# Chunked attention before two feed-forward layers: two heads of a pair on the two row halves of TensorE, shared key rows, whole-width loads in a new order

## Chip, cores and metric

The kernel runs on one core of one Trainium2 chip. The metric is the device time of the program in microseconds; 1169.55 us is the median of three runs before the change (1168.73 to 1170.94).

## What is computed

Attention over chunks of 32 queries, each of which sees 8 memory rows, 16 positions to the left of its chunk, the chunk and 8 positions to the right; then two feed-forward layers on the 3072 x 512 result.

```
B, H, S, D = 4, 8, 768, 64
for each chunk c of 32 queries:
    k_full = concat(mem_k, k[l_start:r_end]); v_full likewise      # 64 rows away from the ends
    a = softmax(q_c @ k_full.T / sqrt(D));   out[c] = a @ v_full
x = out as (3072, 512)
x = (s * relu(x @ w_in)**2 + b) @ w_out                             # d_ff 2048
h = x @ w_in2;  y = (max(h, 0) + alpha * min(h, 0)) @ w_out2
```

The feed-forward weights come as 64-bit floats.

## The kernel before, in words

**Feed-forward.** The 3072 tokens are six blocks of 512 columns. A hidden slice f (128 of 2048) of one block is a unit: G1 (`g1`, L488) is 12 matmuls of 128x512, four pieces of the model dimension by three products of high and low halves (`xh`, `xl` and the two halves of each weight); G2 (`g2`, L547 for layer 0, L549 for layer 1) is 12 more. In between stand `relu` and `square` (ScalarE, L499, L504), `affine` (VectorE, L510, which reads `sb_sb`, loaded by `consts`), `g_high` (ScalarE, L527) and `g_low` (VectorE, L532). There are 2 x 6 x 16 units. Layer 0 begins with slices 0 to 4 of block 0, then the same slices of block 1, then slices 5 to 15 of both; the first two slices of block 0 are done in two halves of 256 columns (`HALVES = 2`).

**Weights.** Each slice's pair of weights is loaded raw (`load_part`, L206) and converted by two ScalarE and five VectorE instructions (`convert`, L218 to L249), the last of which, L249, writes the low half.

**Attention.** A tile is 128 queries of all eight heads of one batch; there are 24, four to a block. Heads go in four pairs. `scores` (L321): for each pair and chunk one matmul with 128 rows (both heads' 64 dimensions), 32 output partitions and 128 columns; its moving operand `kd` holds the two heads' keys on the block diagonal, with zeros elsewhere that `clear` (L282) writes once per buffer. `values` (L388) has the same form with `vd`. Softmax follows on VectorE and ScalarE (`maxima` L333, `shifted` L342, `exps` L346, `sums`, or for the first eight tiles `exps_by_head` L365), `turn` (L376) transposes the probabilities, `normal` (L394) divides, `turn_x` (L402) transposes the result, and `x_high` (L407) and `x_low` (L412) write the tile's columns of `xh` and `xl`. Tiles 0 to 7 (blocks 0 and 1) are done at the start, one buffer set of three each, the sets partly in weight slots. Tiles 8 to 23 are done during layer 0, each in two visits to TensorE between units: `values` of the tile before with `scores` of this one, and later the two transposes.

**Loads.** `kw` and `vw` are loaded as two transfers of 64 partitions each (L304, L310), since each half goes to its own block of the diagonal; `qt` (L301) and the raw weights are transfers of 128 partitions. Every chunk's key window is stored in full, so neighbouring chunks' windows repeat rows.

**Order.** Nothing is scheduled at run time. `Plan.order` lists the steps once, from written costs (the second argument of `plan.add`), ranks and dependencies; each engine then runs its steps in that order. SyncE (SP), which issues the loads, takes its steps strictly by rank. `EARLY_QK`, `EARLY_V` and `EARLY_PARTS` are the ranks of the first loads.

Of the kernel before, what the change touches and what calls it, by code (L numbers as in the profile page):

```python
# [21 lines left out]
HP = H // 2  # L22
NC4 = P // CH
# [12 lines left out]
HALVES = 2  # L36
SPLIT = 2
SETS = 3
EARLY_QK = (-200, -190, -170, -150, -30, -20, -10, 0)
EARLY_V = (-180, -165, -155, -140, -25, -15, -5, 5)  # L40
EARLY_PARTS = {0: -185, 1: -145, 2: -90, 3: -35, 4: -8}
SET_SLOTS = {1: (10, 11, 12), 2: (13, 14, 15)}
# [23 lines left out]
class Plan:  # L66


    PAST = {"PE": 0.25, "DVE": 0.08, "ACT": 0.12, "POOL": 0.12, "SP": 1.8, "PQ": 2.2}
    RATE = 330e3  # L70
# [12 lines left out]
    def order(self):  # L83
# [14 lines left out]
        while len(done) < len(self.steps):  # L98
# [42 lines left out]
            for o in s.outs:  # L141
                o.n_wait -= 1
                o.ready = max(o.ready, at[e] if e == "PE" == o.engine else s.end)
                if not o.n_wait:
                    open_[o.engine].append(o)
# [5 lines left out]
def tile_chunk_attention_two_ffn(ctx: ExitStack, tc: tile.TileContext, qt, kw, vw, win, wout, s1, b1, alpha, out):  # L151
# [16 lines left out]
    plan = Plan({"ph": 2, "g": 2, "gg": 3, "ao": 2, "pa": 2})  # L168
# [33 lines left out]
    def load_part(layer, f, mats):  # L202
        raw = slot_tile(f, mats, [P, len(mats), BLK, 2], U32, "raw")
        raws[layer, f, mats] = raw
        for n, m in enumerate(mats):
            nc.sync.dma_start(out=raw[:, n].rearrange("p n two -> p (n two)"), in_=(win, wout)[m][layer][f])  # L206

    def convert(layer, f, mats, rank, after):
# [41 lines left out]

        early = EARLY_PARTS.get(f, rank - 60) if layer == 0 else rank - 60
        load = plan.add("SP", 0.45 * n, early + 14 * mats[0], lambda: load_part(layer, f, mats), after, nbytes=n * (1 << 19))
        load_done[key] = load
        c0 = plan.add("ACT", 0.22 + 0.43 * n, rank, magnitude, [load], takes=("ao", key))
        c1 = plan.add("DVE", 0.06 + 0.36 * n, rank, clamp, [c0])
        c2 = plan.add("DVE", 0.06 + 0.37 * n, rank, shift, [c1])
        c3 = plan.add("DVE", 0.16 + 0.55 * n, rank, low, [c2])
        c4 = plan.add("DVE", 0.16 + 0.55 * n, rank, sign, [c3])
        hi = plan.add("ACT", 0.2 + 0.43 * n, rank, high, [c4])
        lo = plan.add("DVE", 0.16 + 0.55 * n, rank, rest, [hi], frees=[key])  # L260
# [7 lines left out]
    first_use = {}  # L268

    def make_set(n):  # L270
        shape = [P, 2, HP, NC4, NKEY], [P, 2, NC4, HP, D]
        if n == 0:
            kd, vd = (work.tile(s, F32, tag=t, name=t) for s, t in zip(shape, ("kd", "vd")))
        else:
            kd, vd = (wpool.tile(s, F32, tag=f"w{f}", name=t) for s, f, t in zip(shape, SET_SLOTS[n], ("kd", "vd")))
            sets[n, "qa"] = wpool.tile([P, 2, HP, P], F32, tag=f"w{SET_SLOTS[n][2]}", name="qa")
        sets[n] = kd, vd

    def clear(n, which, par, eng):
        if n not in sets:  # L280
            make_set(n)
        eng.memset(sets[n][which][par * D:par * D + D, 1 - par], 0.0)  # L282

    def pair_tile(n, which, name):
        if n == 0:
            return work.tile([P, HP, P], F32, tag=f"qa{which}", name=name)
        return sets[n, "qa"][:, which]

    def set_of(i):
        return i % SETS if i < 2 * TPB else 0  # L290

# [3 lines left out]
    def load_qk(i):  # L295
# [6 lines left out]
        for par in range(2):  # L302
            r = slice(par * D, par * D + D)
            nc.sync.dma_start(out=sets[n][0][r, par], in_=kw[i, r])  # L304

    def load_v(i):
        n = set_of(i)
        for par in range(2):
            r = slice(par * D, par * D + D)
            nc.sync.dma_start(out=sets[n][1][r, par], in_=vw[i, r])  # L310

    def bank(i, shape, name):
        tag = f"po{i}" if i < TPB else f"pa{held(('att', i))}"
        return psum.tile(shape, F32, tag=tag, name=name)

    def scores(i):
        kd, qT = sets[set_of(i)][0], state[i]["q"]
        sc = bank(i, [P, HP, 2, NKEY], "sc")
# [5 lines left out]
        state[i]["sc"] = sc  # L324

    def maxima(i):
        sc = state[i]["sc"].rearrange("p a two n -> p (a two) n")
        if i % TB == 0:
            nc.vector.memset(sc[0:CH, :, NM:NM + LEFT], NEG)
        if i % TB == TB - 1:  # L330
            nc.vector.memset(sc[P - CH:P, :, NKEY - RIGHT:NKEY], NEG)
        m = small.tile([P, H], F32, tag="m", name="m")
        nc.vector.tensor_reduce(out=m, in_=sc, axis=AX.X, op=ALU.max)  # L333
        state[i]["m"] = m

    def new_e(i):
        state[i]["e"] = pair_tile(set_of(i), 0, "e").rearrange("p a (two n) -> p a two n", two=2)
        return state[i]["e"].rearrange("p a two n -> p (a two) n")

    def shifted(i):  # L340
        sc = state[i]["sc"].rearrange("p a two n -> p (a two) n")
        nc.vector.tensor_tensor(out=new_e(i), in0=sc,  # L342
                                in1=state[i]["m"].unsqueeze(2).to_broadcast([P, H, NKEY]), op=ALU.subtract)
# [4 lines left out]
    def sums(i):  # L348
        rs = small.tile([P, H], F32, tag="rs", name="rs")
        nc.vector.tensor_reduce(out=rs, in_=state[i]["e"].rearrange("p a two n -> p (a two) n"), axis=AX.X, op=ALU.add)  # L350
        state[i]["rs"] = rs

    def negate(i):
        nm = small.tile([P, H], F32, tag="nm", name="nm")
# [3 lines left out]
    def exps_by_head(i, heads):  # L358
        sc = state[i]["sc"].rearrange("p a two n -> p (a two) n")
        if heads[0] == 0:  # L360
            state[i]["er"] = new_e(i)
            state[i]["rs"] = small.tile([P, H], F32, tag="rs", name="rs")
        e, rs = state[i]["er"], state[i]["rs"]
        for h in heads:
            nc.scalar.activation(out=e[:, h, :], in_=sc[:, h, :], func=ACTF.Exp, scale=SCALE,  # L365
                                 bias=state[i]["nm"][:, h:h + 1], accum_out=rs[:, h:h + 1])
# [6 lines left out]
    def turn(i):  # L373
        pt = bank(i, [P, HP, P], "pt")
        for hp in range(HP):
            nc.tensor.transpose(pt[:, hp, :], state[i]["e"][:, hp, :, :].rearrange("p a n -> p (a n)"), ident)  # L376
# [6 lines left out]
    def values(i):  # L383
        vd, aT = sets[set_of(i)][1], state[i]["aT"]
        px = bank(i, [P, HP, 2 * D], "px")
        for hp in range(HP):
            for c in range(NC4):
                nc.tensor.matmul(px[c * CH:(c + 1) * CH, hp, :], lhsT=aT[:, hp, c * CH:(c + 1) * CH],  # L388
                                 rhs=vd[:, :, c, hp, :], start=True, stop=True)
        state[i]["px"] = px  # L390

    def normal(i):
        xn = pair_tile(set_of(i), 1, "xn")
        nc.vector.tensor_tensor(out=xn.rearrange("p a (two d) -> p (a two) d", two=2),  # L394
                                in0=state[i]["px"].rearrange("p a (two d) -> p (a two) d", two=2),
# [476 lines left out]
```

## Time and profile before

| | |
|---|---|
| median of three runs | 1169.55 us (1168.73 to 1170.94) |
| profiled execution, own time | 1167.94 us |
| its span, first to last instruction | 1166.2 us |
| TensorE busy | 1131.6 us, 97% |
| VectorE busy | 612.0 us, 52% |
| ScalarE busy | 354.8 us, 30% |
| DMA moved | 101.66 MB |

Busy time of TensorE counts overlapping matmuls once; a busy TensorE need not be at its peak. A group's row tells line, engine, operation, output<-input, shape and count. In a timeline a row is one instruction or a run of like ones; the time in square brackets is how long the engine sat idle before it, with what released it.

### The profile page before, as it was taken

How to read it: one execution, taken by the hardware profiler on the slowest of the kernel's cores; microseconds unless marked ns; L12 is line 12 of the kernel's file. 1: busy time of each engine (PE TensorE's matmuls, PEld its weight loads, DVE VectorE, ACT ScalarE, POOL GpSimd, SP SyncE). 2: the span in 40 equal slices, each digit the busy share in tenths (PEclk: the TensorE clock that was granted, in tenths of full speed). 3: DMA queues.
4: the chain of work that ended last, by engine and by line, in shares of the span. 5: the costliest groups of instructions: out<-in, count | busy, mean ns of one | idle time of the engine just before them, and what ended most of it. 6: DMA issues, size and time to landing. Idle time of an engine off the chain costs nothing.

```text
span 1166.2 us, 15335 instructions
## 1 busy us (share of the span) xinstructions
PE 1131.6 (97%) x6384; PEld 932.2 (80%) x6384; DVE 612.0 (52%) x932; ACT 354.8 (30%) x653; POOL 34.1 (3%) x64
## 2 busy tenths in 40 slices
PE   4799999999999999999999999999999999999998
PEld 3678778888888888888888788888888888888886
DVE  6695794455445445444588785433433433434433
ACT  4675554433223223223565331111111111111111
POOL 2000000000000000000000000000000000000000
PEclk9899999999999999999999999999999999999999
DMA  9994204426123123203555402001002102000000
GB/s 241 266 326 170 82 1 138 107 68 177 46 60 123 46 64 113 59 19 109 191 206 204 158 1 73 37 1 72 37 1 72 37 1 73 37 1 1 37 1 37
DMA packets 34613, 101.66 MB, mean 87 GB/s; under 512 B 4592, under 2 KB 4592, under 8 KB 34544
## 3 DMA queue, kind: packets, MB, share of 16 engines
q1 hardware_dynamic: 28848, 80.76, 22.7%
q0 software_dynamic: 5696, 19.93, 4.5%
q8 instruction: 50, 0.82, 0.3%
q14 instruction: 19, 0.16, 0.0%
HBM read 79.70 MB, written 20.97 MB: 86 GB/s over the span
## 4 chain that ended last, share of the span: by engine, by line
PE 48%; issue 44%; DMA 4%; ACT 2%; POOL 1%; DVE 1%; SPq 0%; POOLq 0%; ACTq 0%
PE ph L488 23%; PE po L549 22%; DMA kd<-in_kw_dram 2%; PE po L547 2%; POOL x1d L586 1%; DMA raw<-in_wout_dram 1%; PE px L388 0%; DMA qa<-in_qt_dram 0%; ACT qa L365 0%; ACT e L365 0%; DMA x1d<-o 0%; ACT g L499 0%; ACT a L218 0%; PE sc L321 0%; DMA out_dram<-y 0%
## 5 line engine op out<-in xcount | busy, mean ns | idle before, releaser
L488 PE MATMUL ph<-xh,w 128*128 128x512 f32 (+1 forms) x1552 | 508.4, 390 | 1.6 <-DVE w L249 1.6
L488 PEld LDWEIGHTS ph<-xh,w 128*128 128x128 f32 x1552 | 291.4, 188 | 65.2 <-issue 3.2
L488 PE MATMUL ph<-xl,w 128*128 128x512 f32 (+1 forms) x776 | 301.0, 388 | 0.0
L527 ACT ACTIVATE gh<-g 128x512 fp32r<-128x512 f32 (+1 forms) x194 | 121.7, 627 | 467.5 <-DVE g L519 377.7
L547 PE MATMUL po<-gh,w 128*128 128x512 f32 (+1 forms) x784 | 255.3, 387 | 1.2 <-ACT os L559 1.2
L549 PE MATMUL po<-w,gh 128*128 128x512 f32 x768 | 252.4, 391 | 2.6 <-DVE o L583 2.6
L532 DVE TENSOR_TENSOR gl<-g,gh 128x512 fp32r<-128x512 f32 (+1 forms) x194 | 132.9, 685 | 104.4 <-ACT gh L527 103.8
L514 DVE TENSOR_SCALAR g<-ph,alpha_sb 128x512 f32<-128x512 f32 x96 | 72.0, 750 | 211.0 <-PE ph L488 211.0
L547 PEld LDWEIGHTS po<-gh,w 128*128 128x128 f32 x784 | 146.5, 188 | 32.1 <-issue 1.6
L549 PEld LDWEIGHTS po<-w,gh 128*128 128x128 f32 x768 | 144.9, 189 | 33.2 <-DVE o L583 3.0
L488 PEld LDWEIGHTS ph<-xl,w 128*128 128x128 f32 x776 | 146.4, 189 | 28.6
L547 PE MATMUL po<-gl,w 128*128 128x512 f32 (+1 forms) x392 | 151.1, 385 | 1.4 <-DVE gl L532 1.4
L549 PE MATMUL po<-w,gl 128*128 128x512 f32 x384 | 149.9, 390 | 0.0
L499 ACT ACTIVATE g<-ph 128x512 f32<-128x512 f32 (+1 forms) x98 | 57.9, 591 | 144.8 <-PE ph L488 142.9
L547 PEld LDWEIGHTS po<-gl,w 128*128 128x128 f32 x392 | 73.7, 188 | 16.4 <-DVE gl L532 2.2
L549 PEld LDWEIGHTS po<-w,gl 128*128 128x128 f32 x384 | 72.3, 188 | 15.1
L506 DVE TENSOR_TENSOR g<-g 128x512 f32<-128x512 f32 x48 | 33.3, 693 | 77.5 <-ACT g L499 77.3
L510 DVE TENSOR_SCALAR g<-g,sb_sb 128x512 f32<-128x512 f32 (+1 forms) x98 | 52.4, 534 | 39.7 <-ACT g L504 37.8
L519 DVE SCALAR_TENSOR_TENSOR g<-ph,g 128x512 f32<-128x512 f32 x96 | 66.2, 689 | 2.7
L218 ACT ACTIVATE a<-raw 128x1024 f32<-128x1024 f32 (+1 forms) x36 | 37.4, 1039 | 25.3 <-DVE w L249 10.4
L243 ACT ACTIVATE w<-a 128x1024 fp32r<-128x1024 f32 (+1 forms) x36 | 34.7, 963 | 29.9 <-DVE a L236 29.9
L249 DVE TENSOR_TENSOR w<-a,w 128x1024 fp32r<-128x1024 f32 (+1 forms) x36 | 39.6, 1102 | 4.5 <-ACT w L243 4.4
(64 smaller groups left out, 563.1 us busy)
## 6 DMA issues: line engine op xcount, KB each, us to landing
raw<-in_win_dram SPq DMA_DIRECT2D x32, 512.0 KB, 4.6
raw<-in_wout_dram SPq DMA_DIRECT2D x32, 512.0 KB, 5.7
kd<-in_kw_dram SPq DMA_DIRECT2D x48, 256.0 KB, 4.7
vd<-in_vw_dram SPq DMA_DIRECT2D x48, 256.0 KB, 4.8
x1d<-o POOLq DMA_DIRECT2D x24, 512.0 KB, 3.2
xh<-x1d SPq DMA_DIRECT2D x6, 1024.0 KB, 5.6
xl<-x1d SPq DMA_DIRECT2D x6, 1024.0 KB, 7.6
out_dram<-y POOLq DMA_DIRECT2D x20, 256.0 KB, 2.3
```

The costliest lines, as they stand in the source:

```text
L218: nc.scalar.activation(out=temp["a"], in_=words(1).bitcast(F32), func=ACTF.Abs)
L243: nc.scalar.activation(out=w[:, :, 0, :], in_=temp["a"], func=ACTF.Copy)
L249: nc.vector.tensor_sub(out=w[:, :, 1, :], in0=temp["a"], in1=w[:, :, 0, :].bitcast(F32))
L488: nc.tensor.matmul(p, lhsT=w[:, a, kk * P:(kk + 1) * P], rhs=x[:, kk, cols], start=(i == 0), stop=(i == 3 * KD - 1))
L499: nc.scalar.activation(out=new_g(u), in_=ph.pop(u), func=ACTF.Relu)
L510: nc.vector.tensor_scalar(out=g, in0=g, scalar1=sb_sb[:, 0:1], scalar2=sb_sb[:, 1:2], op0=ALU.mult, op1=ALU.add)
L514: nc.vector.tensor_scalar(out=new_g(u), in0=ph[u], scalar1=0.0, scalar2=alpha_sb[:, f:f + 1], op0=ALU.min, op1=ALU.mult)
L519: nc.vector.scalar_tensor_tensor(out=g, in0=ph.pop(u), scalar=0.0, in1=g, op0=ALU.max, op1=ALU.add)
L527: nc.scalar.activation(out=gh, in_=gt[u], func=ACTF.Copy)
L532: nc.vector.tensor_sub(out=gl, in0=gt.pop(u), in1=gh.bitcast(F32))
L547: nc.tensor.matmul(po[d][:, cols], lhsT=w[:, a, ds_], rhs=g, start=start, stop=stop)
L549: nc.tensor.matmul(po[d], lhsT=g[:, ds_], rhs=w[:, a, :], start=start, stop=stop)
```

## The change

The two heads of a pair become two matmuls of 64 rows and 64 columns each, one on each half of the array's rows, that write to two PSUM banks. Neither `kd` nor `vd` has zeros any more, and `clear` is gone. The key window of four chunks is one row of 184 positions, in which a chunk's right context is the next chunk's left one (before, 256). Keys and values load as one transfer of 128 partitions per tile. There are four buffer sets at the start (two of their own, two in weight slots 14 and 15 with slot 13), and two instead of one afterwards. Tiles 0 to 3 use the four `po` banks in pairs, all others one tile `pa` of two banks. The first loads stand in a written list, the first tiles have other ranks, `exps_by_head` is used for tiles 4 to 7 alone, `HALVES` is 1, and the planner's costs differ.

```diff
-HALVES = 2
+HALVES = 1
-SETS = 3
-EARLY_QK = (-200, -190, -170, -150, -30, -20, -10, 0)
+SETS, OWN_SETS = 4, 2
+FIRST_LOADS = """q0 w0i q1 v0 v1 w0o q3 q2 v3 q4 w1i v2 w2 v4 w3 q5 w1o v5 w6 q6 v7 w4 q7 c v6 w7 w5 w9 w8""".split()
+TILE_RANKS = (-130, -90, -85, -115, 0, -30, -25, -10, 0)
+BY_HEAD = (4, 5, 6, 7)
+KROW = NC4 * (CH + NM) + KHEAD
...
     def load_qk(i):
-        for par in range(2):
-            r = slice(par * D, par * D + D)
-            nc.sync.dma_start(out=sets[n][0][r, par], in_=kw[i, r])
+        nc.sync.dma_start(out=sets[n][0], in_=kw[i])
...
     def scores(i, banks=None):
         for hp in range(HP):
             for c in range(NC4):
-                nc.tensor.matmul(sc[c * CH:(c + 1) * CH, hp, :, :].rearrange("p two n -> p (two n)"),
-                                 lhsT=qT[:, hp, c * CH:(c + 1) * CH], rhs=kd[:, :, hp, c, :],
-                                 start=True, stop=True)
+                for par in range(2):
+                    r = slice(par * D, par * D + D)
+                    nc.tensor.matmul(parts[par][c * CH:(c + 1) * CH, 0, hp, :],
+                                     lhsT=qT[r, hp, c * CH:(c + 1) * CH], rhs=kd[r, hp, c * (CH + NM):c * (CH + NM) + NKEY],
+                                     start=True, stop=True)
...
+    def products(prev, i):
+        banks = bank_pair(i, "sp")
+        if i is not None:
+            scores(i, banks)
+        if prev is not None:
+            values(prev, banks)
```

`values` changes as `scores` does. In the order of instructions this shows at three places. First, TensorE at one attention visit of the later tiles; L388 and L415 are `values`, L321 and L335 `scores`, `po` and `ph` the feed-forward around it. Before:

```order
L547 MATMUL po_2589<-gl,w 128x512
L547 MATMUL po_2589<-gh,w 128x512
L388 MATMUL px<-vd,aT 32x128 x16
L321 MATMUL sc<-kd,qT 32x128 x16
L488 MATMUL ph<-xh_75,w 128x512
```

And now:

```order
L616 MATMUL po_2912<-gl,w 128x512
L616 MATMUL po_2912<-gh,w 128x512
L335 MATMUL sp<-kd,qT 32x64 x32
L415 MATMUL sp<-vd,aT 32x64 x32
L557 MATMUL ph<-xh_75,w 128x512
```

Twice the matmuls, each half as wide; the place among the feed-forward matmuls is the same. Second, SyncE's queue of loads up to `consts` (`sb_sb`). Before, its last rows ahead of it:

```order
L304 DMA kd<-in_kw_dram 64x1024 x2
L206 DMA raw<-in_win_dram 128x1024
L310 DMA vd<-in_vw_dram 64x1024 x2
L206 DMA raw<-in_wout_dram 128x1024
L206 DMA raw<-in_win_dram 128x1024
L206 DMA raw<-in_wout_dram 128x1024
L206 DMA raw<-in_win_dram 128x1024
L206 DMA raw<-in_wout_dram 128x1024
L612 DMA sb_sb<-in_s_dram 128x1
```

And now:

```order
L312 DMA qa<-in_qt_dram 128x512
L313 DMA kv<-in_kw_dram 128x736
L318 DMA kv<-in_vw_dram 128x1024
L217 DMA raw<-in_win_dram 128x1024
L217 DMA raw<-in_wout_dram 128x1024
L312 DMA qa<-in_qt_dram 128x512
L313 DMA kv<-in_kw_dram 128x736
L679 DMA sb_sb<-in_s_dram 128x1
```

Ahead of `consts` stood four tiles' queries and keys, four tiles' values and six raw weights; now eight tiles' queries and keys, seven tiles' values and twelve raw weights. Third, VectorE from the first `affine` (L579, before L510) on, now; L250 and L263 are conversion, L601 is `g_low`, L353 `maxima`, L422 `normal`:

```order
L579 TENSOR_SCALAR g<-g,sb_sb 128x256
L250 SCALAR_TENSOR_TENSOR a<-raw,a 128x1024
L391 TENSOR_SCALAR rs<-rs 128x8
L392 RECIPROCAL rs<-rs 128x8
L601 TENSOR_TENSOR gl<-g,gh 128x256
L579 TENSOR_SCALAR g<-g,sb_sb 128x256
L235 TENSOR_SCALAR a<-a 128x1024
L263 TENSOR_TENSOR w<-a,w 128x2x512
L240 TENSOR_SCALAR a<-a 128x1024
L245 SCALAR_TENSOR_TENSOR a<-raw,a 128x1024
L352 MEMSET sp 32x2x4x8
L353 TENSOR_REDUCE m<-sp 128x8
```

From this `affine` to the `x_low` of tile 7 (L454, before L412) VectorE has 63 instructions, conversions of slices 1 to 6 among them; the `affine` is queued ahead of them all.

## Rows read from the trace of the kernel before

**Rows 1.** The page, its head and part 1: busy us, share of the span, instructions.

```profile
span 1166.2 us, 15335 instructions
...
PE 1131.6 (97%) x6384; PEld 932.2 (80%) x6384; DVE 612.0 (52%) x932; ACT 354.8 (30%) x653; POOL 34.1 (3%) x64
```

**Rows 2.** Stretches of the span: busy us of each engine, clock, DMA share, GB/s.

```profile
0.00:83.38 83.38, 59.71 (x733) 48.70 (x734) 61.07 (x113) 52.71 (x184) 6.11 (x12) 0.94 0.96 274
...
170.00:550.00 380.00, 379.74 (x2532) 313.50 (x2531) 178.18 (x308) 120.05 (x201) 8.52 (x16) 1.00 0.29 85
...
670.00:1140.00 470.00, 470.00 (x2075) 389.20 (x2074) 207.11 (x290) 68.00 (x104) 10.80 (x20) 1.00 0.08 30
```

**Rows 3.** Timeline of TensorE, one attention visit: start us, us, instruction.

```profile
320.73 0.39 PE L547 MATMUL po<-gh,w 128*128 128x512 f32 x1
321.04 1.08 PE L388 MATMUL px<-vd,aT 128*32 128x128 f32 x32
321.94 1.06 PE L321 MATMUL sc<-kd,qT 128*32 128x128 f32 x32
322.93 0.50 PE L488 MATMUL ph<-xh,w 128*128 128x512 f32 x1
323.26 0.40 PE L488 MATMUL ph<-xl,w 128*128 128x512 f32 x1
```

**Rows 4.** Stretches inside that visit, `values` alone: PE and PEld instructions at work.

```profile
321.04:321.07 0.03, 0.03 (x4) 0.03 (x4) 0.00 (x0) 1.00 0.00 0
321.07:321.17 0.10, 0.10 (x4) 0.10 (x8) 0.00 (x0) 1.00 0.00 0
321.17:321.20 0.03, 0.03 (x8) 0.03 (x8) 0.00 (x0) 1.00 0.00 0
```

**Rows 5.** The tile `kd`: durations in ns, min/median/max.

```profile
L321 PEld LDWEIGHTS sc<-kd,qa x160: 106/110/178, 9.8 to 69.7; 128*32 128x32 f32 x160
L321 PE MATMUL sc<-kd,qa x160: 269/273/423, 9.8 to 69.8; 128*32 128x128 f32 x160
```

**Rows 6.** Two stretches with different loads under way, columns as in rows 2.

```profile
15.00:20.00 5.00, 3.83 (x63) 2.92 (x65) 3.48 (x9) 3.48 (x12) 0.00 (x0) 1.00 1.05 228
...
66.00:79.00 13.00, 12.65 (x166) 10.24 (x168) 12.01 (x23) 12.44 (x44) 0.00 (x0) 1.00 1.02 409
```

**Rows 7.** Timeline of SyncE: the first load, then loads of those two stretches, and `consts`.

```profile
0.75 0.39 SPq L301 DMA_DIRECT2D qT<-in_qt_dram  x1
...
9.72 4.43 SPq L310 DMA_DIRECT2D vd<-in_vw_dram  x4
...
29.80 0.33 SPq L612 DMA_DIRECT2D sb_sb<-in_s_dram  x1
...
64.12 0.44 SPq L206 DMA_DIRECT2D raw<-in_win_dram  x1
```

**Rows 8.** Timeline of VectorE: the first `affine`, and six instructions back to back.

```profile
40.12 0.41 DVE L510 TENSOR_SCALAR g<-g,sb_sb 128x256 f32<-128x256 f32 x1 [0.71 <-ACT a L218]
...
43.79 0.40 DVE L510 TENSOR_SCALAR g<-g,sb_sb 128x256 f32<-128x256 f32 x1
44.11 0.68 DVE L226 TENSOR_SCALAR a<-a 128x1024 uint32<-128x1024 uint32 x1
44.72 0.68 DVE L333 TENSOR_REDUCE m<-sc 128x8 f32<-128x512 f32 x1
45.32 1.21 DVE L231 SCALAR_TENSOR_TENSOR a<-raw,a 128x1024 uint32<-128x1024 uint32 x1
46.45 0.16 DVE L355 TENSOR_SCALAR nm<-m 128x8 f32<-128x8 f32 x1
46.56 1.22 DVE L236 SCALAR_TENSOR_TENSOR a<-raw,a 128x1024 uint32<-128x1024 uint32 x1
```

**Rows 9.** Two more stretches, columns as in rows 2.

```profile
40.00:60.00 20.00, 15.88 (x187) 13.97 (x185) 14.91 (x28) 13.52 (x50) 0.00 (x0) 1.00 1.01 236
60.00:80.00 20.00, 18.80 (x241) 14.85 (x231) 18.82 (x34) 16.17 (x50) 0.00 (x0) 1.00 0.91 348
```

**Rows 10.** Timeline of TensorE: the first matmul of block 1.

```profile
83.22 0.39 PE L488 MATMUL ph<-xh,w 128*128 128x512 f32 x1
```

**Rows 11.** TensorE's waits from 83 to 200 us: in total, times, longest.

```profile
PE po L547 <- DVE gl L532: 1.4, 2, 1.2
PE po L547 <- ACT os L559: 1.2, 1, 1.2
PE ph L488 <- DVE w L249: 1.1, 2, 0.7
```

**Rows 12.** The same from 200 us to the end, the longest.

```profile
PE po L549 <- DVE o L583: 2.6, 1, 2.6
PE px L388 <- DMA vd<-in_vw_dram: 0.2, 1, 0.2
```

More of the change, by code (lines that the diff above doesn't have):

```diff
@@ L316, in scores, with bank_pair @@
-    def scores(i):
+        if set_of(i) not in sets:
+            make_set(set_of(i))
+        nc.sync.dma_start(out=sets[set_of(i)][1], in_=vw[i])
+    def bank_pair(i, name):
+        if i in ALONE:
+            return [psum.tile([P, 2, HP, D], F32, tag=f"po{2 * ALONE[i] + par}", name=name) for par in range(2)]
+        both = psum.tile([P, 2, 2, HP, D], F32, tag="pa", name=name)
+        return [both[:, par] for par in range(2)], both
+    def scores(i, banks=None):
         kd, qT = sets[set_of(i)][0], state[i]["q"]
-        sc = bank(i, [P, HP, 2, NKEY], "sc")
+        banks = banks or bank_pair(i, "sc")
+        parts, both = banks if isinstance(banks, tuple) else (banks, None)
@@ new lines, in scores, with pieces @@
+        state[i]["sc"] = pieces(parts, both, 0)
+    def pieces(parts, both, which):
+        if both is not None:
+            return [(slice(0, 2), both[:, :, which])]
+        return [(slice(par, par + 1), parts[par][:, which:which + 1]) for par in range(2)]
+    def maxima(i):
+        m = small.tile([P, 2, HP], F32, tag="m", name="m")
+        for pars, sc in state[i]["sc"]:
+            if i % TB == 0:
+                nc.vector.memset(sc[0:CH, :, :, 0:LEFT], NEG)
+            if i % TB == TB - 1:
+                nc.vector.memset(sc[P - CH:P, :, :, NKEY - RIGHT:NKEY], NEG)
+            nc.vector.tensor_reduce(out=m[:, pars], in_=sc, axis=AX.X, op=ALU.max)
@@ L419, in attention, with loads @@
+    def loads(i, r):
         n = set_of(i)
+        left = leaves.get(n, {})
         early = i < 2 * TPB
[L421 to L424 removed]
         a = att[i] = {}
[L426 to L432 removed]
@@ L461, in finish_tile @@
[L461 to L471 removed]
+        a["lq"] = plan.add("SP", 0.9, first_load(f"q{i}") if early else r - 15, lambda: load_qk(i), [left.get("k"), left.get("e")], nbytes=P * 4 * (HP * P + HP * KROW))
@@ new lines, in attention @@
+    def attention(prev, i, r, r2):
+        after = []
+        if i is not None:
+            loads(i, r)
+            after.append(att[i]["lq"])
+        if prev is not None:
+            after += [att[prev]["aT"], att[prev]["lv"]]
+        both = plan.add("PE", 0.2 + 0.5 * len([t for t in (i, prev) if t is not None]), r,
+                        lambda: products(prev, i), after + list(banks_free.get("pa", [])))
+        after = []
+        if prev is not None:
+            finish_values(prev, r, both)
+            after.append(att[prev]["xn"])
+        if i is not None:
+            leaves[set_of(i)]["k"] = both
+            softmax(i, r, both)
+            after.append(att[i]["e"])
+        both = plan.add("PE", 0.1 + 0.43 * len(after), r2, lambda: turns(prev, i), after + [id_])
+        free = []
+        if prev is not None:
+            free.append(finish_tile(prev, r2, both))
+        if i is not None:
+            finish_turn(i, r2, both)
+            free.append(att[i]["aT"])
+        banks_free["pa"] = free
@@ L636, in tile_chunk_attention_two_ffn @@
     done_po = [None] * KD
-    for i in range(TPB):
-        done_po[i] = x_done[i]
+    for d in range(KD):
+        done_po[d] = banks_free.get(d // 2)
     reads = {}
```

314 lines of the change are left out of this document (149 added, 165 removed).

## The prediction

> **What bounds it now.** I read the page's shares first [rows 1]: TensorE is busy for 97% of the span, VectorE for half, so almost everything is TensorE's own work. The stretches [rows 2] say where that fails. From 670 to 1140 us TensorE does 2075 matmuls in 470 us, 0.2265 us each, without a gap; 4608 of that width are 1043.7 us of the 1166.2. From 170 to 550 us it is as full, but attention visits stand between the units. And in the first 83.4 us it has 733 instructions at work for 59.7 us, most of them attention's: that is where the rest lies. So a change can gain in three places: cheaper visits, a shorter start, and the few waits that are left [rows 11, 12].
>
> A visit [rows 3]: the last wide matmul before it starts at 320.73 and the second one behind it at 323.26, 2.53 us in which two wide ones (0.45) pass, so 2.08 us go to 32 matmuls, which the profile records as 64. Inside it [rows 4], four records are at work in the first 0.03 us, none is added in the next 0.10, and four join at 321.17: four column strips work at once, and a strip's next record starts 0.11 us after its last. At 321.94 less 321.04, `values` takes 0.90 us for eight such rounds.
>
> The start is bound by loads, then by VectorE. While value halves arrive (four were issued from 9.72 us on, [rows 7]) the DMA engines are full at 228 GB/s; while raw weights arrive they are full at 409 [rows 6]. The 64-partition transfers run at little more than half the rate of the 128-partition ones. VectorE is busy for 14.9 of the 20 us from 40 on, and 18.8 of the next 20 [rows 9]. The first matmul of block 1 starts at 83.22 [rows 10], for want of the last early tile; 108 wide matmuls' worth of feed-forward stand before it in TensorE's order.
>
> **Part 1, the visits of tiles 8 to 23.** Sixteen visits, each 32 matmuls of 128 columns before, 64 of 64 columns now, on eight places of the array instead of four. If the halves work at once, a round is eight records in half of 0.11 us, and 16 rounds take 0.87 in place of 1.74 us. Two things could hold it back. Records have to be issued: four fit in 0.03 us [rows 4], so eight fit in about 0.055, just the round. And weights have to be in place: a weight load's record lasts 110 ns [rows 5], as long as today's round, which could mean that it sets it. But the second four loads are at work by 321.07 to 321.17 together with the first [rows 4], so most of a record is travel, not occupation. From both sides: 0.95 us saved a visit if the ends shrink too, nothing if the halves take turns. I take 0.85, nearer the upper end, since the four strips already overlap fully: 16 x 0.85 = **13.6 us**, all on the path, as TensorE is full from 170 to 550. The transposes' visits are unchanged. VectorE and ScalarE get the same instructions per later tile over the same 512 columns; they are busy for only 178 and 120 us of the 380 there [rows 2].
>
> **Part 2, the start.** Keys shrink from 512 to 368 KB a tile, and every load now has 128 partitions. Both pull the loads forward, but the new list puts `consts` behind 8 x 639 KB of queries and keys, 7 x 524 KB of values and 12 x 524 KB of weights: 15.07 MB. The first `affine` needs it, VectorE runs in order, and the 62 instructions behind it wait with it. Loads begin to move about 2 us in (an estimate: the first is issued at 0.75 us, [rows 7]); 15.07 MB at 409 GB/s are 36.9 us, and with its own travel `consts` lands near **40 us**. Whether VectorE is ready for it by then the rows don't say; before, the first `affine` ran at 40.12 [rows 8], with far less loaded.
>
> [...]
>
> From the first `affine` to tile 7's `x_low` VectorE has 63 instructions. Back to back (starts in [rows 8]) a 512-wide one (or a 1024-wide one with one input) takes 0.60 us, a 1024-wide one with two inputs 1.13, a 256-wide one 0.32, a small one 0.11: 26 x 0.60, 14 x 1.13, 10 between 0.32 and 0.46, and 13 small ones are 37.1 us. They won't run without gaps; from 60 to 80 us VectorE was 94% busy, from 40 to 60, short of loads, 75% [rows 9]. At 92%, near the upper one because loads are ahead now, that is 40.3 us: block 1 can start at **80.3 us** instead of 83.2. By then the new order has 120 wide matmuls' worth done (slices 0 to 4 of block 0 complete) instead of 108, 12 x 0.2265 = 2.7 us more. Against it, TensorE has nothing left of block 0 to do while the first slice of block 1 goes through ScalarE and VectorE: about 1 us. Gain 2.9 + 2.7 - 1 = **4.6 us**. Ends: `consts` at 38.4 and no gaps give 75.5 us, a gain of 9.4; a VectorE at 75% gives 89.5, a loss of 4.6. The removed clears stood before the first scores and freed only idle time; fewer exponentials by head (four tiles instead of eight) cut ScalarE's queue inside the same bound.
>
> **Part 3, waits from 83 to 200 us.** They add up to 3.7 us [rows 11], two kinds of them on VectorE's conversions. From tile 7 on VectorE has 55.7 us of work to the last conversion, priced as above, while TensorE has 15 units of 5.44 us, 81.6: conversion gets well ahead. I take **3 us** gained, between 0 and 3.7.
>
> **Part 4, the passage between the layers.** TensorE waits 2.6 us for a copy of block 5's result [rows 12]. The order there now has 12 wide matmuls (2.7 us) fewer between the last G2 of layer 0 and that wait. If the copies come no sooner the wait grows by 2.7; if they ride on TensorE's earlier units, not at all. I take **1.5 us** lost.
>
> Edits priced at nothing: one half-slice fewer, the second buffer set (from 200 us on a load was waited for once, for 0.2 us [rows 12]) and bank use, all beside TensorE's full queue; without that cover a later tile's load would cost a few us once.
>
> Sum against the profiled span: 1166.2 - 13.6 - 4.6 - 3.0 + 1.5 = 1146.5, so 1148.2 for the profiled execution's own 1167.94. The median of the runs is 1.6 us above that one, so I forecast 1169.55 - 19.7 = **1150 us**. A difference under 0.2% (2.3 us) is about what the runs can't tell from none.
>
> **Rivals.** *Halves take turns.* Scores and values of two heads share strips and, if the array runs one row half at a time, a visit keeps its 2.08 us: 1150 + 13.6 = 1163.5. For it: nothing in the trace shows two row halves at once. Against it: strips overlap, rows 4.
>
> *Slow loads.* If the rate belongs to these tensors and not to half-width transfers, 15.07 MB at 236 GB/s [rows 9] are 63.9 us, `consts` lands at 67, block 1 starts at 107: 24 us later, less 2.7, plus 1. With the other parts 1169.55 + 22.3 - 13.6 - 3 + 1.5 = 1177. Against it: raw weights and queries, both 128 wide, come at the full rate.
>
> *One record after another.* Twice the instructions on TensorE cost more than their width saves. Today a record costs 0.90 / 32 = 28 ns on average; if that is the price of a record and not a quarter of a round, 128 records take 3.5 us in place of 1.8 and each visit is 1.7 us longer: 1169.55 + 27.5 - 4.6 - 3 + 1.5 = 1191, slower. It decides from 15 ns a record upward. The bunching in rows 4 speaks against it. The Trainium skill, "TensorE: Matmul & The Clock Gate", Wait — 56ns, not 53.3ns?, puts the distance between matmul starts at 25 ns or more however narrow they are, which would be this case; four starts within 0.03 us [rows 4] disagree.
>
> *A freer start.* VectorE without gaps behind early constants: 1150 - 5 = 1145 or somewhat less.
>
> **How the numbers follow.** Forecast 0.76 (its own range 1142 to 1157), a freer start 0.08, turns 0.08, slow loads 0.05, one after another 0.03. The favourable ends of all parts give 1169.55 - 9.4 - 15 - 3.7 = 1141; a little below that to just under the case of turns is 1139 to 1162. Faster 0.91 (forecast, free start, turns, less a little for a start gone wrong), slower 0.07, same 0.02.
>
> **What would show it.** In the profile after: a `scores` of about 0.45 us with eight records to a round, visits 0.8 to 0.9 us shorter; the DMA engines near 400 GB/s from 3 to 40 us; the first `affine` right behind the landing of `consts` near 40 us; the first matmul of block 1 near 80 us; no wait of note from 83 to 200 us; a wait of 3 to 5 us between the layers. Wrong would be: rounds that keep 0.11 us with eight records, a start whose VectorE sits idle for something other than `consts`, or a later stage with new waits.

## Result, and the profile after

The changed kernel takes 1157.43 us (median of four runs, 1156.37 to 1161.06), against 1170.24 us for the kernel before in the same comparison (four runs): a ratio of 0.9896, with a 95% interval of 0.9870 to 0.9922. That is 12.8 us off, where 19.7 were forecast; 1157.4 lies inside the stated range of 1139 to 1162 and just outside the forecast's own, 1142 to 1157. The profiled executions, from which the steps below are read, are 1157.31 and 1167.94 us, 10.6 apart; their spans 1155.5 and 1166.2.

The page's head, and its part 1, against [rows 1]:

```profile
span 1155.5 us, 18208 instructions
...
PE 1124.4 (97%) x7896; PEld 925.9 (80%) x7896; DVE 617.3 (53%) x941; ACT 349.7 (30%) x590; POOL 28.7 (2%) x58
```

TensorE has 24% more records and is busy for 7 us less. VectorE has as much to do as before. Where the time went shows when the start of the same wide matmul is looked up in both traces (counted in 512-wide ones; the two orders do other attention in between, so a row is good to a visit or so until the last visit at 513 us):

| wide matmuls begun | before, us | after, us | difference |
|---|---|---|---|
| 108 | 83.22 | 77.20 | -6.0 |
| 120 | 85.94 | 86.70 | +0.8 |
| 192 | 102.26 | 105.75 | +3.5 |
| 2280 | 629.55 | 622.16 | -7.4 |
| 2400 | 660.44 | 650.49 | -10.0 |
| 3000 | 797.13 | 786.49 | -10.6 |

So the start lost 3.5 us (2.7 of them between matmuls 120 and 192), the stretch with the sixteen visits gained 10.9, the passage between the layers 3.3, and behind it nothing moved.

**The visits.** The timeline of TensorE at one visit of the changed kernel, to be held against [rows 3]:

```profile
315.86 0.39 PE L616 MATMUL po<-gh,w 128*128 128x512 f32 x1
316.18 0.80 PE L335 MATMUL sp<-kd,qT 64*32 64x64 f32 x60
316.76 0.24 PE L415 MATMUL sp<-vd,aT 64*32 64x64 f32 x1
316.77 0.22 PE L335 MATMUL sp<-kd,qT 64*32 64x64 f32 x1
316.78 0.24 PE L415 MATMUL sp<-vd,aT 64*32 64x64 f32 x1
316.79 0.25 PE L335 MATMUL sp<-kd,qT 64*32 64x64 f32 x3
316.84 0.82 PE L415 MATMUL sp<-vd,aT 64*32 64x64 f32 x62
317.59 0.50 PE L557 MATMUL ph<-xh,w 128*128 128x512 f32 x1
317.93 0.39 PE L557 MATMUL ph<-xl,w 128*128 128x512 f32 x1
```

From 315.86 to 317.93, less two wide ones, are 1.62 us, 0.46 less than before and not 0.85; the other full visits agree within 0.01 us. In the middle one half of the rows is already at `values` while the other is still at `scores`: the halves do work at once. The same timeline cut off at 316.42 shows the pace at the beginning:

```profile
316.18 0.45 PE L335 MATMUL sp<-kd,qT 64*32 64x64 f32 x32
```

32 records start in 0.24 us, about 7 ns apart, which is close to the forecast's round of eight in 0.055 us. The other 96 start from 316.45 to 317.45: but for a few short breaks a record starts every 16.7 ns in each half. Over the whole visit a record takes 10 ns.

**The start.** Its loads run at the full rate, and TensorE's clock is at its lower level (half of 2.4 GHz) for the second stretch:

```profile
10.00:20.00 10.00, 6.05 (x216) 4.78 (x215) 8.64 (x23) 4.43 (x8) 0.00 (x0) 1.00 1.03 400
20.00:30.00 10.00, 6.37 (x186) 5.89 (x191) 5.17 (x14) 3.25 (x7) 0.00 (x0) 0.51 1.03 406
```

The chain of waits of the start (start us, us, what; lines left out):

```profile
19.05 0.32 PE sp L335 x10
19.37 2.41 issue
21.77 1.04 PE sp L335 x49
...
26.04 1.86 issue
...
33.27 0.84 issue
34.11 0.53 PE px L415 x11
34.63 0.02 issue
34.65 0.33 SPq L318
...
37.93 0.43 SPq L679
...
38.40 5.81 DMA sb_sb<-in_b_dram
...
44.31 0.41 DVE g L579
```

TensorE stands still three times, for 5.1 us in all, with no engine and no load to wait for ("issue"; in the trace of before there is one such wait up to 60 us, of 2.6). Between two of these waits it has worked through about 255 records of matmuls and weight loads:

```profile
21.76:26.03 4.27, 4.26 (x127) 4.01 (x128) 2.46 (x8) 1.52 (x3) 0.00 (x0) 0.50 1.04 411
```

TensorE's instructions arrive over the DMA engines in packets of 16 KB, 62 for 15,792 such records in this trace, so about 256 records to a packet. The waits fall where a packet is used up: they are waits for instructions. By them and the lower clock tile 3's `values` (L415) end at 34.6. SyncE's queue holds the load of tile 7's values (L318) until then, because it goes into the same buffer, and everything behind it waits too, `consts` (L679) included:

```profile
SPq L318 <- PE px L415: 5.7, 1, 5.7
```

They are issued at 37.93 and land at 44.2, and only then comes the first `affine`. Block 1 starts at 86.70 (83.22 before, [rows 10]), for want of the last tile:

```profile
86.70 0.79 PE L557 MATMUL ph<-xh,w 128*128 128x512 f32 x1 [0.69 <-ACT xh L449]
```

This matmul takes 0.79 us and not 0.39, since the clock is at its lower level again. From 81.3 to 86.7 us TensorE stood idle three times, 3.5 us in all; the clock fell at 85.1 and rose at 91.9:

```profile
87.00:90.00 3.00, 3.00 (x7) 2.10 (x7) 1.73 (x3) 1.27 (x2) 0.54 (x1) 0.50 0.69 229
```

The 12 matmuls from 120 on take 5.4 us in place of 2.7. That is the step from +0.8 to +3.5 in the table; before, the clock was at its upper level there.

**The passage between the layers.** TensorE's longest wait for a copy of block 5, in place of the 2.6 us of [rows 12]:

```profile
PE po L618 <- DVE o L652: 0.8, 1, 0.8
```

### The profile page after: what moved, and what is told of

Same layout as the page of the kernel before. It is cut to its first block, busy times and chain, and to the rows that moved or that the text cites. A ratio compares the mean times of both kernels' runs of the same rounds, so it can differ in the third digit from the quotient of the medians.

```text
span 1155.5 us, 18208 instructions
## 1 busy us (share of the span) xinstructions
PE 1124.4 (97%) x7896; PEld 925.9 (80%) x7896; DVE 617.3 (53%) x941; ACT 349.7 (30%) x590; POOL 28.7 (2%) x58
## 4 chain that ended last, share of the span: by engine, by line
PE 59%; issue 29%; DVE 6%; DMA 2%; ACT 1%; POOL 1%; SPq 0%; POOLq 0%; DVEq 0%; ACTq 0%
PE ph L557 29%; PE po L618 22%; PE po L616 6%; DVE a L250 1%; DMA kd<-in_kw_dram 1%; DVE w L263 1%; DVE a L245 1%; DVE gl L601 1%; POOL x1d L655 1%; DMA x1d<-o 1%; DVE a L235 1%; DMA sb_sb<-in_b_dram 1%; DVE a L240 0%; DVE g L579 0%; PE pt L400 0%
## 5 line engine op out<-in xcount | busy, mean ns | idle before, releaser
L601 DVE TENSOR_TENSOR gl<-g,gh 128x512 fp32r<-128x512 f32 (+1 forms) x193 | 132.5, 687 | 105.6 <-ACT gh L596 105.2
L579 DVE TENSOR_SCALAR g<-g,sb_sb 128x512 f32<-128x512 f32 (+1 forms) x97 | 52.5, 542 | 49.7 <-ACT g L573 45.0
L263 DVE TENSOR_TENSOR w<-a,w 128x1024 fp32r<-128x1024 f32 (+1 forms) x36 | 39.5, 1099 | 2.9 <-ACT w L257 2.9
```

The costliest lines, as they stand in the source:

```text
L263: nc.vector.tensor_sub(out=w[:, :, 1, :], in0=temp["a"], in1=w[:, :, 0, :].bitcast(F32))
L579: nc.vector.tensor_scalar(out=g, in0=g, scalar1=sb_sb[:, 0:1], scalar2=sb_sb[:, 1:2], op0=ALU.mult, op1=ALU.add)
L601: nc.vector.tensor_sub(out=gl, in0=gt.pop(u), in1=gh.bitcast(F32))
```

## The experiments

Each comparison has its own runs of the kernel before (medians 1169.4 to 1170.8 us), and times are medians unless said otherwise. Where a stage is discussed, it is read from the same matmul's start in the traces, as in the table above.

### One row half after the other

```diff
-        for hp in range(HP):
-            for c in range(NC4):
-                for par in range(2):
+        for par in range(2):
+            for hp in range(HP):
+                for c in range(NC4):
...
```

(The same in `values`.)

> Edit: in scores and values all matmuls of the one row half come first, then all of the other; nothing else changes. After the change a later visit costs 1.62 us (the last wide matmul before it starts at 315.86, the second behind it at 317.93, less two wide ones), 0.46 less than before where 0.85 was forecast. Inside it the first 32 records start 6.8 ns apart, the rest as two streams, one for each row half, in each of which a record starts every 16.7 ns. Theory A (instructions: once what had been fetched ahead is used up, a matmul reaches the array every 16.7 ns, whichever half it is for; one half alone is then held by its columns, 64 of them in four strips, 13.6 ns a record): 128 x 13.6 ns and 0.35 at the ends are 2.09 us a visit, 0.47 more than now, 16 visits 7.5 us: about 1165 us. Theory B (weight loads: a load keeps a row half for 16.7 ns): one half after the other is 128 x 16.7 ns and the ends, 2.49 us a visit, 14 us in all: about 1171 us, records 16.7 ns apart throughout. Theory C (the halves never worked at once, the gain came from narrower keys): no difference.

1163.37 us (0.9937, 0.9915 to 0.9958). A visit:

```profile
319.65 0.39 PE L616 MATMUL po<-gh,w 128*128 128x512 f32 x1
319.97 0.92 PE L335 MATMUL sp<-kd,qT 64*32 64x64 f32 x60
...
321.63 0.50 PE L557 MATMUL ph<-xh,w 128*128 128x512 f32 x1
321.97 0.40 PE L557 MATMUL ph<-xl,w 128*128 128x512 f32 x1
```

319.65 to 321.97 less two wide ones is 1.87 us, 0.25 more than after the change, where theory A said 0.47 and B 0.87. One half alone starts three records 16.7 ns apart and a fourth 6 ns later, four in 56 ns: 14 ns a record, what its columns need (half of the 0.11 us of [rows 4] for four strips). So B, by which no half ever goes faster than 16.7, is out, and so is C. A's 0.47 was too much because the halves still overlap where the queue changes from one to the other. The total is 5.9 us longer; 16 x 0.25 are 4.0 of it, and 2.0 were lost in the start.

### Half as many columns

```diff
+        width = D if i < 2 * TPB else D // 2
...
-                    nc.tensor.matmul(parts[par][c * CH:(c + 1) * CH, 1, hp, :], lhsT=aT[r, hp, c * CH:(c + 1) * CH],
-                                     rhs=vd[r, c, hp, :], start=True, stop=True)
+                    nc.tensor.matmul(parts[par][c * CH:(c + 1) * CH, 1, hp, :width], lhsT=aT[r, hp, c * CH:(c + 1) * CH],
+                                     rhs=vd[r, c, hp, :width], start=True, stop=True)
```

> Edit: from tile 8 on scores and values take 32 columns instead of 64, so half of the keys and half of the value columns are left out; two wide matmuls ahead of each visit write the banks first. Theory A (both halves at work are held by the supply of instructions, a matmul of two records every 16.7 ns, 8.35 ns a record): the visit's 128 records behind the first 32 keep 16.7 ns in each half, the visit loses about what it does now, 1.5 to 1.6 us beside the two wide ones. Theory D (columns, with some loss where the halves meet): records come 8 to 9 ns apart in each half and the visit loses 0.9 to 1.1 us.

One execution, 1165.21 us.

```profile
371.39 0.61 PE L440 MATMUL sp<-w 128*128 128x512 f32 x2
371.93 0.72 PE L336 MATMUL sp<-kd,qT 64*32 64x32 f32 x62
...
372.50 0.75 PE L417 MATMUL sp<-vd,aT 64*32 64x32 f32 x62
373.18 0.50 PE L563 MATMUL ph<-xh,w 128*128 128x512 f32 x1
373.51 0.39 PE L563 MATMUL ph<-xl,w 128*128 128x512 f32 x1
```

The second of the two wide ones ahead starts at 371.61, so the visit is 373.51 - 371.61 - 0.45 = 1.45 us, hardly less than 1.62 with half the columns. The first 32 records start in 0.16 us, faster than before; behind them the pace is again 16.7 ns in each half, with both halves' records now starting together. It does not hang on the columns, so theory D is out. Weight loads don't set it by themselves either: the first 32 records bring theirs along and start 5 to 7 ns apart. Theory A is left: what paces a visit of small matmuls is how fast TensorE is handed them, two records every 16.7 ns for the two halves together, once those that had queued up ahead are used up. No run shows the handing over itself, and which part of the way sets the pace stays open.

### The old costs

```diff
-    RATE = 390e3
+    RATE = 330e3
...
-        c1 = plan.add("DVE", 0.07 + 0.27 * n, rank, clamp, [c0])
+        c1 = plan.add("DVE", 0.06 + 0.36 * n, rank, clamp, [c0])
...
```

> Edit: the planner's costs and delays of the kernel before for conversion, units, spills and copies; loads, row halves and the attention steps' own costs stay as they are now. Theory A (the 3.5 us gained between 97 and 630 us beside the visits and the 3.3 us at the passage between the layers come from the new costs, by which copies and conversions stand elsewhere): both come back, 600 to 660 us loses about 3 us and 100 to 200 us about 3, total 1162 to 1165 us. Theory B (they come from attention that is out of VectorE's way earlier, and the costs change nothing that is waited for): within 1.5 us of 1157.4.

1162.10 us (0.9924, 0.9903 to 0.9945). The wait between the layers is back to the length of [rows 12]:

```profile
PE po L618 <- DVE o L652: 2.6, 1, 2.6
```

From matmul 2280 to 3000 this kernel loses 3.2 us against the changed one, the whole gain of that passage: theory A there. At matmul 480 it is only 1.4 us behind what it was at 192, and has that back by 1600. So the waits from 100 to 200 us are mostly gone for another reason than the costs. Theory B, that conversion and attention are further ahead by then, fits; no run tests it by itself.

### Two transfers of 64 partitions

```diff
-        nc.sync.dma_start(out=sets[n][0], in_=kw[i])
+        for par in range(2):
+            r = slice(par * D, par * D + D)
+            nc.sync.dma_start(out=sets[n][0][r], in_=kw[i, r])
```

(The same for `vw`.)

> Edit: keys and values load as two transfers of 64 partitions each, as before the change, with the same bytes. Theory A (a transfer of 64 partitions runs at 228 GB/s where one of 128 runs at 409): of the 15.07 MB ahead of consts 6.6 MB then take 13 us more, though the wait for a buffer at 28.6 to 34.65 hides some; consts land at 50 to 56 instead of 43.4, block 1 starts 6 to 12 us later, total 1163 to 1170. [...]

1179.21 us (1.0064, 1.0041 to 1.0086), slower than before the change. The same stretches as above, and VectorE's first `affine`:

```profile
10.00:20.00 10.00, 6.44 (x193) 5.05 (x196) 7.32 (x18) 3.27 (x6) 0.00 (x0) 1.00 1.04 254
20.00:30.00 10.00, 6.35 (x233) 4.94 (x218) 5.87 (x15) 2.16 (x4) 0.00 (x0) 1.00 1.04 248
```

```profile
62.72 0.42 DVE L583 TENSOR_SCALAR g<-g,sb_sb 128x256 f32<-128x256 f32 x1 [13.61 <-DMA sb_sb<-in_b_dram]
```

The engines are as full and move 250 GB/s instead of 400. VectorE stands still for 13.6 us, and block 1 starts at 106.0, 19.3 us later. Theory A, and more than it said; if the low rate of before had belonged to other loads under way, the engines would have stayed near 400 GB/s. The Trainium skill, "DMA: Bandwidth & Descriptors", Rules for kernel authors, advises one transfer of 128 partitions in place of two to the partition halves. The trace agrees: 400 GB/s for 250. The whole order of loads of this change lives on the whole-width transfers: with it and without them the kernel would have become slower.

### Consts first

```diff
         nc.sync.dma_start(out=sets[set_of(i)][1], in_=vw[i])
+        if i == 1:
+            consts()
...
-    cs = plan.add("SP", 1.3, first_load("c"), consts)
+    cs = plan.add("SP", 1.3, first_load("c"), lambda: None)
```

> Edit: the three small loads of consts are issued right behind the second tile's values instead of behind 15 MB of loads; the order of everything else stays word for word. Now VectorE waits 2.9 us for them, its first affine runs at 44.31, and block 1 starts at 86.70. Theory A (VectorE's queue behind that affine sets block 1's start, and consts come late because SyncE's queue was held from 28.6 to 34.65 us by a values load that needs a buffer): the affine follows the instruction before it at about 41.4, block 1 starts at about 83.8 and the time is 2.9 us shorter, about 1154.5. Theory B (the last tile's own chain through TensorE, ScalarE and the one pair of banks sets it, VectorE only fills the time): the affine is early, block 1 still starts at 86 to 87, no difference beyond 1 us.

1155.67 us (0.9872, 0.9851 to 0.9892), 1.8 less than after the change. The two intervals overlap; in the traces wide matmul 192 starts 1.8 us earlier too. VectorE:

```profile
42.72 0.41 DVE L581 TENSOR_SCALAR g<-g,sb_sb 128x256 f32<-128x256 f32 x1
...
50.00 0.11 DVE L354 MEMSET sp<- 32x64 f32 x1 [1.21 <-PE sp L417]
```

The `affine` no longer waits, but 7 us later VectorE waits for TensorE, whose clock was at the lower level until 44.7 us. Block 1 starts at 85.81, 0.9 earlier; the other 0.9 comes because the clock is back sooner behind that. Theory A holds for 1.6 of its 2.9 us (the `affine`, from 44.31 to 42.72); then another chain takes over.

### Late slices, and both

```diff
-        c0 = plan.add("ACT", 0.02 + 0.51 * n, rank, magnitude, [load], takes=("ao", key))
+        late = [x_done[2 * TPB - 1]] if layer == 0 and f >= SEG else []
+        c0 = plan.add("ACT", 0.02 + 0.51 * n, rank, magnitude, [load] + late, takes=("ao", key))
```

> Edit: the conversion of slices 5 and up waits for tile 7's x_low; the rest of the order follows from that. Now VectorE is busy without a gap to speak of from 50 to 82 us, and ten of its instructions there, 8.2 us, belong to slices 5 and 6, which nobody needs before block 1 has done its first five slices (27 us). Theory A (VectorE's length of queue sets block 1's start): block 1 starts 4 to 8 us earlier than at 86.7, the conversions fit behind it, total 1150 to 1154 us. Theory B (the last tiles' chain through one pair of banks sets it, conversions only fill VectorE's gaps): block 1 starts within 1 us of 86.7 and the time stays within 1 us of 1157.4, or is longer if slice 5 then comes late.

> Edit: late slices and early consts together. The early consts alone gave 1.8 us of the 2.9 expected, since behind the affine VectorE next waited 1.2 us for values on a TensorE at half clock. Theory A (VectorE's queue): the two gains add up to 6 to 10 us, total 1148 to 1151. Theory B (the chain of the last tiles): about 1155 to 1156, as with early consts alone.

Alone 1158.46 us (0.9906, 0.9888 to 0.9924), with early consts 1155.43 (0.9884, 0.9862 to 0.9905). By their totals both are theory B. Taking 8.2 us of conversion out of VectorE's queue ahead of tile 7 moves block 1's start by 0.1 us alone. With early consts it moves by 3.5 us instead of 0.9, so there VectorE's queue does hold it, as theory A had it; but 1.4 are lost again by 130 us, and the total is that of early consts alone.

### TensorE filled

```diff
+    def warm(n):
+        p = psum.tile([P, BLK], F32, tag="ph1", name="junk")
+        for k in range(n):
+            nc.tensor.matmul(p, lhsT=xl[1][:, 0, :P], rhs=xl[1][:, 0, :], start=(k == 0), stop=(k == n - 1))
...
```

> Edit: three wide matmuls on a zeroed buffer, whose result nobody reads, behind each transpose and each values of tiles 0 to 3, where TensorE waits for a copy or a division anyway. Now the granted clock falls to half at 20.9 us, after a gap in which TensorE waits 2.4 us for instructions, and comes back at 44.1. Theory A (the half clock follows from too little work on TensorE, and what it costs is TensorE's part of the chain from 21 to 44 us): with the filling the clock stays or comes back by 35 us, the first affine comes near 40 us instead of 44.3 unless consts hold it, block 1 starts 1 to 4 us earlier, total 1153 to 1157. Theory B (the clock does not matter there, loads and VectorE set the pace): the clock may rise but the added matmuls cost their own 12 x 0.7 us where a step is ready early, total 1157 to 1162.

1162.29 us (0.9936, 0.9912 to 0.9961), just past theory B's range. The clock fell at 24 us all the same, behind an "issue" wait of 3.06 us, and a second one of 3.19 followed, both longer than any after the change. From 36 to 44 us the clock was at its upper level, without a gain in time: wide matmul 24 starts at 49.16, after the change at 45.73. Whether the clock alone would help stays open, since the added matmuls cost time and instructions of their own.

### Loads held back

```diff
-FIRST_LOADS = """q0 w0i q1 v0 v1 w0o q3 q2 v3 q4 w1i v2 w2 v4 w3 q5 w1o v5 w6 q6 v7 w4 q7 c v6 w7 w5 w9 w8""".split()
+FIRST_LOADS = """q0 w0i q1 v0 v1 w0o q3 q2 v3 w1i v2 w1o c gate q4 w2 v4 w3 q5 v5 w6 q6 v7 w4 q7 v6 w7 w5 w9 w8""".split()
...
+    plan.add("SP", 0.5, first_load("gate"), lambda: nc.sync.dma_start(out=x1d[0][:, 0, 0, :4].bitcast(F32), in_=xl[0][:, 0, 3 * P:3 * P + 4].bitcast(F32)), [x_done[TPB - 1]])
```

> Edit: only the loads that tiles 0 to 3 and slices 0 and 1 need are issued at first (and consts); all others wait behind a small transfer that needs tile 3's x_low. So the DMA engines are idle from about 18 us until then. Now TensorE waits for instructions three times in the start, 2.41, 1.86 and 0.84 us, and each time goes on 2.3 to 2.5 us after a packet of 16 KB of instructions began (19.32, 25.55, 31.68 us). The time will be far longer, as the later loads start 15 to 20 us late; only TensorE's waits are asked for. Theory A (instructions come late because the loads fill the engines): with idle engines the waits in that stretch shrink to under 0.5 us each. Theory B (the time of such a fetch is its own, and dense small matmuls use up 16 KB faster than it takes): the waits stay at 1 to 2.5 us, idle engines or not.

One execution, 1162.38 us. Two stretches of it, and TensorE's waits from 18 to 36 us, the longest ones:

```profile
10.00:18.00 8.00, 5.59 (x177) 4.41 (x167) 6.28 (x17) 3.66 (x6) 0.00 (x0) 1.00 1.03 406
18.00:30.00 12.00, 8.73 (x300) 7.28 (x284) 10.75 (x28) 5.89 (x11) 0.00 (x0) 0.86 0.18 60
```

```profile
PE sc L335 <- DVE xl L454: 1.8, 1, 1.8
PE ph L557 <- ACT xh L449: 1.1, 1, 1.1
PE px L415 <- ACT qa L405: 0.7, 1, 0.7
```

The same view of the changed kernel begins with three other rows:

```profile
PE sp L335 <- issue: 2.4, 1, 2.4
PE ph L557 <- issue: 1.9, 1, 1.9
PE px L415 <- issue: 0.8, 1, 0.8
```

With idle DMA engines TensorE does not wait for instructions, though packets of them come as before (16 KB at 19.64, 23.45 and 27.57 us, which take 0.9 to 1.3 us each, as with full engines). What differs is when they begin: 3.8 and 4.1 us apart, where after the change it was 6.2 and 6.1 (19.32, 25.55, 31.68 us). So the second and the third begin well before TensorE has run dry. The first tells nothing, as TensorE waits for VectorE at that point (1.8 us). The clock is 0.86 from 18 to 30 us, and wide matmul 24 starts at 39.66 instead of 45.73. The list has consts and slice 1 earlier too, but early consts alone (46.74) and the list in order of need below (49.69) don't bring that. This is theory A, as far as the spacing of the fetches goes. And although the loads of tiles 4 to 7 wait until 33 us (from 10.19 on after the change), this one execution is only 5 us longer.

### Orders that start sooner

Consts early and slices 2, 3 and 4 loaded ahead of 5 and 6; the same with late slices; and the last one, with the hold of the experiment above, but only until tile 1's `x_low`:

```diff
+FIRST_LOADS = """q0 w0i q1 v0 v1 w0o q3 q2 v3 q4 w1i v2 w2 v4 w1o q5 w3 v5 w4 q6 v7 q7 c v6 w5 w6 w7 w8 w9""".split()
```

(The edits for consts and late slices are those above.) In the last version the list is this one, with `c` for consts and `gate` for the hold:

```diff
+FIRST_LOADS = """q0 w0i q1 v0 v1 w0o q3 q2 v3 w1i v2 w1o c gate q4 w2 v4 q5 w3 v5 w4 q6 v7 q7 v6 w5 w6 w7 w8 w9""".split()
```

> Edit: consts early, and the list of first loads in the order of need: slices 2, 3, 4 ahead of 5 and 6, where now slice 6 comes before 4. With early consts alone 1155.7 us; the chain of what ended last there went through the second raw matrix of slice 4, which was issued at 51 and landed at 59.5 us. Theory A (that load sets VectorE's pace behind 50 us): slice 4 is converted up to 5 us earlier, block 1 starts 2 to 4 us earlier than with early consts alone (85.8), total 1152 to 1154. Theory B (VectorE's own length of queue from 50 to 82 us): 1155 to 1156.

> Edit: that list, early consts, and the conversion of slices 5 and up behind tile 7's x_low. With early consts and late slices on the old list 1155.4 us, block 1's second unit 3.9 us earlier than after the change, 1.4 of it lost again at 130 us. Theory A (loads of slice 4 were next): block 1 starts at 79 to 82 us, total 1151 to 1154. Theory B (TensorE's own waits for instructions and its half clock are next, no order of loads helps): 1155 to 1156.

> Edit: as with the list in order of need and late slices, but with the hold: loads beyond tiles 0 to 3 and slices 0 and 1 wait for tile 1's x_low (about 21.5 us) instead of tile 3's, so that the engines are idle for some 3 us where TensorE's first wait for instructions stood. With the long hold there was no such wait at all and the 24th wide matmul came 6 us earlier than after the change, at 39.7, but the later slices' weights then came late (5.3 us at one wait) and the time was 1162. Theory A (the waits for instructions cost more at the start than the loads lose by 3 us of idle engines): block 1 starts at 79 to 82 us, total 1150 to 1154. Theory B (weights become late as with the long hold, or the fetches at 23 and 27 us wait as before): 1155 to 1160.

1156.57 us (0.9879, 0.9855 to 0.9902), 1154.74 (0.9867, 0.9845 to 0.9890) and 1152.39 (0.9849, 0.9829 to 0.9869). The list alone is theory B, worth nothing beside early consts. With late slices it lies between the theories: block 1 starts at 83.32. The last version beats the changed kernel; the two intervals, each against the kernel before, just fail to meet. Its block 1 starts at 81.94, 4.8 us earlier, as theory A said. But the waits for instructions are not gone:

```profile
PE px L416 <- issue: 4.2, 2, 3.7
PE sc L336 <- DVE xl L455: 1.8, 1, 1.8
PE sc L336 <- issue: 0.8, 1, 0.8
```

They add up to 5.0 us, as after the change, at other places: the longest, 3.7, now comes when the loads run again. The first falls into the hold. Its packet began at 20.49 us, the engines moved 26 GB/s, and TensorE went on only 2.35 us later:

```profile
20.50:22.50 2.00, 0.33 (x11) 0.17 (x11) 2.00 (x5) 1.45 (x4) 0.00 (x0) 0.94 0.08 26
...
22.84 1.08 PE L336 MATMUL sc<-kv,qa 64*32 64x64 f32 x53 [0.76 <-issue]
```

So from the beginning of its packet a fetch takes this long of itself, as theory B of the held loads had it, and idle engines did not shorten that. The result is the theory A of this version and its mechanism isn't. Which of its four edits carries it stays open; the version with three of them, without the hold, gains 2.7 us of the 5.0.

## Why the prediction was right or wrong

**Part 1, the visits**: right in kind, half in size, 16 x 0.46 = 7.4 us instead of 13.6. The step that failed is "Records have to be issued: four fit in 0.03 us [rows 4], so eight fit in about 0.055, just the round". It was read from four records that had been waiting in the queue, and it holds for just such records: the first 32 of a visit. A visit now has 128, and the rest come at 16.7 ns in each half. The rival of one record after another asked the right question, the price of a record, and put the threshold at 15 ns (its own 1.8 us over 128 records are 14); 10 ns were measured, which costs half the gain but doesn't turn the sign. The halves do not take turns.

**Part 2, the start**: the wrong sign, 3.5 us lost instead of 4.6 gained, 8.1 apart. The rate of the loads was right, 400 GB/s for the 409 taken, and the start that the rival of slow loads worked out is the one that two transfers each give: block 1 at 106.0, for 107. Three steps failed. "`consts` lands near **40 us**" was worked out from bytes and rate alone; SyncE takes its queue in order, and a load in front of `consts` needed a buffer that TensorE gave back at 34.6. So the first `affine` ran at 44.31, 4.3 us late. VectorE then took 42.4 us to tile 7's `x_low` (86.68) where 40.3 were taken, 2.1 more. And behind block 1's start no wait came, for which 1 us had been taken, but 2.7 us were lost to the clock, for which there is no term: 1.7 more. Early consts show 1.8 us of the 8.1, in about equal parts from an earlier start of block 1 and from the clock; with 1155.7 us they alone don't make the freer start of the rival, 1145.

Under the late `affine` lies another missing term. Attention's matmuls, twice as many, were priced at nothing in the start; TensorE waited 5.1 us there for instructions (2.6 before), with the clock at its lower level from 20 to 44 us. What these waits cost by themselves is not shown: in the one run without them wide matmul 24 starts 6.1 us sooner, with other loads moved too, and the last version has as many microseconds of them and starts block 1 4.8 us sooner. The 12 wide matmuls done ahead were right: 120 stand before block 1.

**Part 3**: right. 10.9 us from matmul 192 to 2280, less 7.4 for the visits, leaves 3.5, for a forecast of 3, and no wait is left from 100 to 200 us. It does not come from the new costs; that it comes from conversion that is ahead, as forecast, is argued.

**Part 4**: the wrong sign, 3.3 us gained for 1.5 lost. "The order there now has 12 wide matmuls (2.7 us) fewer" was counted on TensorE alone; the new costs also place the copies elsewhere among the conversions on ScalarE and VectorE. The last copy starts 26.6 us after wide matmul 2280, in place of 28.7 before and with the old costs. TensorE's longest wait is 0.8 us instead of 2.6. Behind the longer wait the clock fell for a while (0.91 from 650 to 670 us), now it doesn't (1.00).

Two errors of 8.1 and 6.2 us against and two of 4.8 and 0.5 in favour: the total came out 9 us from the forecast in the span. It lies inside the stated range because that reached up to the case that holds back the halves, and because Part 4, by luck, went the other way.

## What to carry to other kernels

When a matmul is cut into smaller ones, price the instructions and not only the columns: read the pace of a record late in a long run of them, not in its first few. In a stage where loads keep the DMA engines full, more instructions for TensorE are more fetches, and each begins later behind those loads. An idle stretch of TensorE can cost twice, the second time by the clock behind it. A small load that an in-order engine needs first belongs ahead of every load that may wait for a buffer, however few its bytes.

## What the runs showed of the hardware that was not expected

Small matmuls on both row halves start 5 to 7 ns apart for the first 32 records of a visit and then, but for short breaks, every 16.7 ns in each half, with 64 columns or 32. The Trainium skill, "TensorE: Matmul & The Clock Gate", Architectural detail: the array is 16× 32×32, not 1× 128×128, gives TensorE a queue of 64 instructions. 32 records with a weight load each are 64, so the trace agrees, in every visit.

TensorE's instructions come in packets of 16 KB through the same DMA engines as the data. After the change, with the engines full, the packets began 6.2 and 6.1 us apart, and TensorE went on 2.45, 2.34 and 2.43 us after such a packet began (19.32, 25.55, 31.68 us), of which it stood still for 2.41, 1.86 and 0.84. With idle engines they began 3.8 and 4.1 us apart. The 2.3 us and more from packet to going on stayed with idle engines too (2.35 in the last version).

Loads with keys and values in transfers of 64 partitions moved 250 GB/s, all in 128 partitions 400, with the engines full both times, in otherwise the same program.
